# A quarter-row block of the query weights loaded onto 28 partitions by chosen DMA engines

## The chip, the cores and the metric

The kernel runs on one core of a Trainium2 chip. The time is device microseconds of one execution; three executions of the kernel before took 195.91, 196.07 and 196.13 us, median 196.07. A further execution was recorded by the hardware profiler; all times inside the kernel come from it, counted from its first instruction.

## The reference

One decode step of a gated mix of two blocks, for 4 batch rows with one token each, all in bf16:

```python
g = sigmoid((x * gate_w).sum(-1, keepdims=True))
q = (x @ wq)                     # 4 x 512 by 512 x 4096: 32 heads of 128
k, v = the last 4096 of 16384 cached rows, 8 heads, each for 4 query heads
o = softmax(q k^T * 128 ** -0.5) v
a = o @ wo                       # 4 x 4096 by 4096 x 512
b = (relu(x @ W_gate) * (x @ W_up)) @ W_down
return g * a + (1 - g) * b
```

Nearly all bytes are the caches: 32 pairs of batch row and cache head, each 4096 x 128 for K and again for V, 64 MiB in all. Weights add some 13 MiB. Each byte is read once and takes part in a few multiplications only.

## The kernel before

**Sets and slots.** The 32 pairs are done in eight sets of four heads of one batch row. A set's K and its V are one load of 4 MiB each, a partition holding 32 KB. Four slots of that size (`slots`, L109) are used in turn by every large load: query weights, K 0, K 1, V 0, K 2, V 1 and so on, then the gate and up weights together, V 7, the down weights and the output weights. `_dma_order` (L159) lists the loads and `_slots` (L166) gives each its slot and the event that frees it: the last transpose of a K, the last matmul of a V, the second half of the query matmuls for the query weights.

**Queues.** SyncE (SP) issues every load, in that order, on one queue (`sync`, L252); it waits where a slot is not free yet. A load of 128 partitions is spread over the core's sixteen DMA engines, eight partitions each, and every engine takes its part of the queue's loads one after the other. A load counts as landed when all its engines' parts have. The output weights come in five pieces (`WO_PIECES`, L28) that get smaller, so that the last matmuls can follow the last bytes closely. The fifth, 512 bytes a partition, is cut by `LOW3` (L29) into partitions 0 to 122, 123 to 125 and 126 to 127, which makes three transfers of it.

**The order of the work.** `_order` (L147) is one list that every compute engine follows, each through its own part. Ahead of the sets:

- GpSimd (POOL) builds identity matrices, masks and folding matrices, each step waiting for the one before (L287).
- VectorE (DVE) clears the block-diagonal query buffer `qblk` and the PSUM banks (`INIT`, L485).
- TensorE (PE) makes three constants from POOL's, then transposes x and the gate vector, five rows in all, in four pieces of 128 (`XT`, L333). Row 4p+t of the query weights sits on partition p as its t-th quarter, hence the step of four in the transposes.
- `Q` (L344): the query matmuls, two halves of 2048 columns. A half is four blocks of 512 columns times four t, accumulated over t into one PSUM bank, and the four blocks go to the rows from 0, 32, 64 and 96 of that bank.
- The queries are then copied, transposed and put into `qblk` (`EQ`, `QT`, `EQT`).

Within a set DVE transposes K in four fills (`EKT`, L489), PE multiplies them by the queries (`SC`), DVE adds the mask and keeps maxima, ScalarE (ACT) takes the exponential, DVE transposes it, and PE multiplies by V (`PV`). At the end come the second block (`GU`, `FFN`), the folding of the heads (`OQ`) and the output matmuls piece by piece (`WO`, L424): piece p is x from lo to hi, one matmul of 256 columns each. Two copies (`FIN` of ACT and of DVE) and one store end the kernel.

Of the kernel before, what the change touches and what calls it, by code (L numbers as in the profile page):

```python
# [24 lines left out]
OUTT = 2  # L25
OW = 512 // OUTT
OR = 128 // OUTT
WO_PIECES = ((0, 34), (34, 52), (52, 60), (60, 63), (63, 64))  # L28
LOW3 = (0, 123, 126, 128)  # L29

class _Plan:

# [70 lines left out]
def _alloc(nc, ctx):  # L103
    R = {}

    def sb(name, shape, dt):
        R[name] = ctx.enter_context(nc.sbuf_tensor(name, shape, dt))

    sb("slots", [128, NSLOT, 16384], BF16)  # L109
    sb("kt", [128, 4, 4096], BF16)  # L110
    sb("sc", [128, 2048], BF16)
    sb("pe", [128, 2048], BF16)
    sb("pT", [128, 2, 2048], BF16)
    sb("qblk", [128, NSET, 2, 144, 2], BF16)
    sb("xsb", [5, 512], BF16)
    sb("xT", [128, 20], BF16)
    sb("osb", [128, NSET, 512], BF16)
    sb("oq", [128, 32, 4], BF16)
    sb("identb", [128, 128], BF16)
    sb("identf", [128, 128], FP32)  # L120
    sb("ones", [128, 128], FP32)
    sb("ee", [16, 128], BF16)
    sb("e4", [16, 128], BF16)
    sb("rfold", [128, 128], FP32)
    sb("grpb", [128, 128], BF16)
    sb("own8", [128, 8], FP32)
    sb("scl", [128, 8], FP32)
    sb("maskl", [128, 128], BF16)
    sb("maskr", [128, 512], BF16)
    sb("maskf", [128, 512], BF16)  # L130
    sb("gwB", [128, 4, 128], BF16)
    sb("fold", [128, 4, 4, 64], BF16)
    sb("mx4", [128, 4], FP32)
    sb("rd32", [128, 8, 4], BF16)
    sb("negmax", [128, 2], FP32)
    sb("rowsum", [128, NSET], FP32)
    sb("recip", [128, 4, 4], FP32)
    sb("ge", [128, 2, 4], FP32)
    sb("gp", [128, 2, 4], FP32)
    sb("gg", [128, 2, 4], FP32)  # L140
    sb("hg", [128, 14, 4], BF16)
    sb("osum", [4, 512], BF16)
    R["psum"] = ctx.enter_context(nc.psum_tensor("bank", [128, 8, 512], FP32))
    return R
# [12 lines left out]


def _dma_order():  # L159
    o = [("wq",), ("x",), ("gw",), ("k", 0), ("k", 1), ("v", 0)]  # L160
    for s in range(2, NSET):
        o += [("k", s), ("v", s - 1)]
    return o + [("wg",), ("wu",), ("v", NSET - 1), ("wd",)] + [("wo", p) for p in range(len(WO_PIECES))]


def _slots():  # L166

    frees = [[] for _ in range(NSLOT)]
    at, wait = {}, {}
    turn = 0  # L170
    for it in _dma_order():
        k = it[0]
        if k in ("x", "gw") or (k == "wo" and it[1] > 0):
            continue
        if k == "wu":
            at[it] = at[("wg",)]
            wait[it] = wait[("wg",)]
            continue
        n = turn % NSLOT
        turn += 1  # L180
        at[it] = n
        wait[it] = list(frees[n])
        frees[n] = {"k": [("E", "KT", it[-1], 3)], "v": [("PV", it[-1])], "wq": [("Q", 1)], "wg": [("GU", 1)], "wd": [], "wo": []}[k]
    return at, wait


def _program(nc, plan, R, aps):
# [14 lines left out]
    def slot(*it):  # L202
        return slots[:, at[it], :]

    Wq = slot("wq").rearrange("p (t f) -> p t f", t=4)
    Wg, Wu = slot("wg")[:, 0:4 * FF], slot("wg")[:, 4 * FF:8 * FF]
    Wd = slot("wd")[:, 0:14 * 512]
    Wo = slot("wo", 0)
# [26 lines left out]
    def scb(key):  # L235
        return SCB[scf[key] % NSC]
# [2 lines left out]
        n = scf[key] - NSC  # L239
        return [("E",) + sck[n]] if n >= 0 else [("INIT",)]  # L240

    def wo_rows(p):

        return [slice(a, b) for a, b in zip(LOW3, LOW3[1:])] if p == len(WO_PIECES) - 1 else [slice(0, 128)]

    def set_of(s):
        return s % 4, s // 4
# [4 lines left out]
    def sync(e):  # L252
        E = _Eng(plan, e, "sp")

        def load(ev, ctr, dst, src, waits=()):
            E.op(lambda: e.dma_start(dst, src), ev=ev, waits=waits, ctr=ctr)  # L256

        for it in _dma_order():
            k = it[0]
            w = slot_wait.get(it, [])  # L260
            if k == "x":
                load(("X",), "d_x", xsb[0:4, :], A_x.rearrange("b o d -> (b o) d"))
            elif k == "gw":
                load(("GW",), "d_gw", xsb[4:5, :], gate_w.rearrange("(o p) -> o p", o=1))
            elif k == "wq":
                load(("WQ",), "d_wq", slot("wq"), A_wq.rearrange("(p t) f -> p (t f)", t=4), waits=w)
            elif k == "wg":
                load(("WG",), "d_wg", Wg, B_W_gate.rearrange("(p t) f -> p (t f)", t=4), waits=w)
            elif k == "wu":
                load(("WU",), "d_wu", Wu, B_W_up.rearrange("(p t) f -> p (t f)", t=4), waits=w)  # L270
            elif k == "wd":
                load(("WD",), "d_wd", Wd, B_W_down.rearrange("(p i) c -> p (i c)", i=14),
                     waits=w)
            elif k == "wo":
                lo, hi = WO_PIECES[it[1]]
                wo = A_wo.rearrange("(p i) c -> p (i c)", i=32)
                for n, r in enumerate(wo_rows(it[1])):
                    load(("WO", it[1], n), f"d_wo{it[1]}", Wo[r, OW * lo:OW * hi], wo[r, OW * lo:OW * hi], waits=w)
            else:
                b, qq = set_of(it[1])  # L280
                src = (A_k_cache if k == "k" else A_v_cache)[b, 4 * qq:4 * qq + 4, SK - WIN:SK, :]
                load((k.upper(), it[1]), f"d_{k}{it[1] % 3}", slot(*it), src.rearrange("h (r c) d -> r h (c d)", r=32),
                     waits=w)
        load(("OUT",), "d_out", out.rearrange("b o d -> (b o) d"), osum[:, :], waits=[("OSUM", 1), ("OSUM", 0)])
        E.wait([("OUT",)])

    def gpsimd(e):  # L287
# [7 lines left out]
        def aff(dst, src, pattern, base, cmp, fill, ev, mult=1):  # L295
            op(lambda: e.affine_select(dst, src, pattern, cmp, fill, base=base, channel_multiplier=mult), ev)  # L296
# [2 lines left out]
        op(lambda: e.memset(ones[:, :], 1.0), ("ONES",))  # L299
        aff(identf[:, :], ones[:, :], [[-1, 128]], 0, eq, 0.0, ("IDF",))  # L300
        aff(identb[:, :], ones[:, :], [[-1, 128]], 0, eq, 0.0, ("IDB",))
        aff(R["ee"][:, :], ones[0:16, :], [[0, 8], [-1, 16]], 0, eq, 0.0, ("EE",))
        aff(R["e4"][:, :], ones[0:16, :], [[0, 2], [-1, 16], [0, 4]], 0, eq, 0.0, ("E4",))
        op(lambda: e.memset(R["maskl"][:, :], -BIG), ("ML0",))
# [11 lines left out]
    def tensor(t):  # L316
# [16 lines left out]
        def XT():  # L333
            bk = bankb[tr(("XT",))]
            for q in range(4):
                tp(bk[:, 6 * q:6 * q + 5], xsb[0:5, q:q + 509:4], identb[0:5, 0:5], ev=("XT",) if q == 3 else None,
                   waits=tr_free(("XT",)) + [("X",), ("GW",), ("IDB",)])

        def Z():
            for q in range(4):  # L340
# [3 lines left out]
        def Q():  # L344
            for n in range(2):
                key = ("Q", n)
                for q in range(4):
                    for j in range(4):
                        c = (4 * n + j) * 512
                        mm(banks[scb(key)][32 * j:32 * j + 4, :], xT[:, 5 * q:5 * q + 4], Wq[:, q, c:c + 512],  # L350
                           q == 0, q == 3, ev=key if (q, j) == (3, 3) else None, pos=(0, 32 * j),
                           waits=sc_free(key) + [("WQ",), ("E", "XT"), ("INIT",)] if (q, j) == (0, 0) else ())

        def QT():
            for n in range(2):
# [67 lines left out]

        def WO(p):  # L424
            lo, hi = WO_PIECES[p]
            w = [("WO", p, n) for n in range(len(wo_rows(p)))] + [("E", "OQ")]
            for x in range(lo, hi):
                i, j = x // OUTT, x % OUTT
                mm(banks[ACC][OR * j:OR * j + 4, 0:OW], oq[:, i, :], Wo[:, OW * x:OW * x + OW], False, i == 31,
                   ev=("WOP", p) if x == hi - 1 else None, waits=w if x == lo else (), pos=(0, OR * j))  # L430

# [6 lines left out]
    for it in order:  # L438
# [3 lines left out]
        elif k == "CONST":  # L442
            act.append(("ECONST", it[1]))
        elif k == "XT":
            dve.append(("EXT",))
            act.append(("GWB",))
        elif k == "Z":
            act.append(("GE",))
# [33 lines left out]
    def vector(v):  # L482
        E = _Eng(plan, v, "dve")

        def INIT():  # L485
            E.op(lambda: v.memset(qblk[:, :, :, :, :].rearrange("p s h c e -> p (s h c e)"), 0.0), ev=("QZ",))  # L486
            E.op(lambda: v.memset(R["psum"][:, SCB[0]:ACC + 1, :].rearrange("p k c -> p (k c)"), 0.0), ev=("INIT",))

        def EKT(s, f):  # L489
            w = [("K", s)] + ([("SC", s - 1, f)] if s else [])  # L490
            E.op(lambda: v.transpose(kt[:, f, :].bitcast(FP32), slot("k", s)[:, 4096 * f:4096 * f + 4096].bitcast(FP32)),  # L491
                 ev=("E", "KT", s, f), waits=w)

        def EXT():
            E.op(lambda: v.tensor_copy(xT[:, :].rearrange("p (q c) -> p q c", q=4), bankb[tr(("XT",))][:, 0:24].rearrange("p (q c) -> p q c", q=4)[:, :, 0:5]), ev=("E", "XT"), waits=[("XT",)])  # L495

        def EQ(n):
            key = ("Q", n)
# [77 lines left out]
        def FIN():  # L576
            E.op(lambda: v.tensor_copy(osum[:, OW:2 * OW], banks[ACC][OR:OR + 4, 0:OW]), ev=("OSUM", 1),  # L577
                 waits=[("WOP", len(WO_PIECES) - 1)])

        fns = dict(INIT=INIT, EKT=EKT, EXT=EXT, EQ=EQ, G=G, EQT=EQT, ESC=ESC, MAX=MAX, ESW=ESW, EPT=EPT, ERS=ERS, EOQ=EOQ, H=H,  # L580
                   EHT=EHT, FIN=FIN)
        for it in dve:
            fns[it[0]](*it[1:])
# [75 lines left out]
```

## Time and profile before

| What | us |
|---|---|
| median of three executions | 196.07 |
| the profiled execution's own time | 196.06 |
| its span, first to last instruction | 194.8 |
| DVE busy | 124.1 |
| PE busy | 120.6 |
| ACT busy | 27.5 |
| POOL busy | 9.5 |

The span is what the profile covers; the remaining 1.26 us of the profiled execution lie around it. Busy times are sums over an engine's instructions. The page cuts the span into 40 slices of 4.87 us and gives each a digit for the busy share in tenths; the DMA row is the mean over the sixteen engines. Where a window is asked for, the same share is given as a fraction, so that one engine of sixteen counts 0.06. A line of the timeline has start, duration, engine, line, operation, what is written and read, and in brackets the idle time before and what ended it. A line of the waits has who waited, for whom, the time in total, how many times, and the longest.

### The profile page before, as it was taken

Reading aid. Unit: us, or ns where it says so; the run is one execution under the profiler, and the core shown is the slowest. Engines: PE = TensorE matmul, PEld = TensorE weight load, DVE = VectorE, ACT = ScalarE, POOL = GpSimd, SP = SyncE. Lnnn points to the kernel's source line nnn. Section 1 sums busy time; section 2 is a strip of 40 time slices with the busy share of each in tenths; the row PEclk is TensorE's granted clock in tenths of the full one; section 3 lists DMA queues with packets and bytes.
Section 4 is the critical chain, followed back from the end, with each engine's and each line's share of the span. In section 5 each row is a group of like instructions: output and inputs, shape, how many; then the busy total and the mean of one; then the engine's idle time right before and its main releaser. Section 6 shows DMA issues by size and latency. Waiting matters only on the chain.

```text
span 194.8 us, 1734 instructions
## 1 busy us (share of the span) xinstructions
PE 120.6 (62%) x723; PEld 50.6 (26%) x723; DVE 124.1 (64%) x153; ACT 27.5 (14%) x34; POOL 9.5 (5%) x25
## 2 busy tenths in 40 slices
PE   0209279474943894686468943894586466743974
PEld 0003123121411341242112411341142122311562
DVE  6103769999399809980998199819981998370010
ACT  2213000040130013001300130013001300420100
POOL 7830000000000000000000000000000000000000
PEclk9999958999999797899876999697999889997899
DMA  6999999999999999999999999999999999999992
GB/s 215 431 432 431 437 437 431 431 427 451 431 437 437 446 427 424 431 437 431 431 431 431 427 424 437 444 437 431 431 431 421 431 395 427 470 431 384 425 404 90
DMA packets 3616, 81.10 MB, mean 416 GB/s; under 512 B 401, under 2 KB 666, under 8 KB 794
## 3 DMA queue, kind: packets, MB, share of 16 engines
q1 hardware_dynamic: 3610, 81.01, 97.3%
q8 instruction: 5, 0.08, 0.2%
q14 instruction: 1, 0.01, 0.0%
HBM read 81.01 MB, written 0.00 MB: 416 GB/s over the span
## 4 chain that ended last, share of the span: by engine, by line
DMA 54%; DVE 31%; PE 9%; issue 4%; SPq 0%; ACT 0%
DMA slots<-in_A_k_cache_dram 38%; DVE kt L491 21%; DMA slots<-in_A_wo_dram 10%; PE bank L320 7%; DMA xsb<-in_A_x_dram 6%; DVE sc L527 5%; DVE qblk L517 1%; PE bank L324 1%; DVE pT L542 1%; DVE rd L531 1%; SPq L256 0%; DVE negmax L537 0%; ACT gwB L600 0%; DVE osum L577 0%; DVE mx L527 0%
## 5 line engine op out<-in xcount | busy, mean ns | idle before, releaser
L491 DVE STREAM_TRANSPOSE kt<-slots 128x2048 f32<-128x2048 f32 x32 | 73.7, 2305 | 28.1 <-DMA slots<-in_A_k_cache_dram 28.0
L320 PE MATMUL bank<-kt,qblk 128*128 128x512 bf16 x256 | 72.1, 434 | 27.9 <-DVE kt L491 27.9
L320 PEld LDWEIGHTS bank<-kt,qblk 128*128 128x128 bf16 x256 | 25.2, 107 | 69.7 <-DVE kt L491 36.0
L320 PE MATMUL bank<-slots,pT 128*64 128x512 bf16 x256 | 32.3, 410 | 5.7 <-DMA slots<-in_A_v_cache_dram 5.7
L619 ACT ACTIVATE pe<-sc,negmax 128x2048 bf16<-128x2048 bf16 x8 | 16.0, 2002 | 60.1 <-DVE negmax L537 60.1
L527 DVE CUSTOM_DVE_ANT_0 sc<-bank,maskf 128x512 bf16<-128x512 f32 x32 | 21.0, 658 | 3.8 <-PE bank L320 3.7
L320 PEld LDWEIGHTS bank<-slots,pT 128*64 128x64 bf16 x256 | 15.1, 118 | 23.2 <-issue 13.4
L542 DVE STREAM_TRANSPOSE pT<-pe 128x2048 bf16<-128x2048 bf16 x8 | 18.5, 2312 | 2.2 <-ACT pe L619 2.2
L604 ACT ACTIVATE osb<-bank 128x512 bf16<-128x512 f32 x8 | 4.8, 597 | 81.5 <-PE bank L320 81.5
L320 PE MATMUL bank<-rd,grpb 128*128 128x32 bf16 x8 | 1.6, 194 | 22.1 <-DVE rd L531 22.1
L555 DVE TENSOR_TENSOR oq<-bank,recip 64x128 bf16<-64x128 f32 x2 | 0.9, 434 | 12.3 <-PE bank L320 12.2
L320 PEld LDWEIGHTS bank<-rd,grpb 128*128 128x128 bf16 x8 | 0.8, 98 | 25.7 <-DVE rd L531 25.7
L495 DVE COPY xT<-bank 128x20 bf16<-128x20 bf16 x1 | 0.2, 171 | 8.0 <-PE bank L324 8.0
L320 PE MATMUL bank<-slots,oq 128*4 128x256 bf16 x64 | 4.0, 272 | 2.0 <-DMA slots<-in_A_wo_dram 2.0
L320 PE MATMUL bank<-slots,xT 128*4 128x512 bf16 (+1 forms) x64 | 5.0, 467 | 0.0
L320 PE MATMUL bank<-maskr,maskl 128*128 128x512 bf16 x1 | 0.6, 609 | 5.9 <-POOL maskr L296 5.9
L517 DVE TENSOR_SCALAR qblk<-bank 32x64 uint32<-32x64 uint32 x16 | 2.9, 215 | 2.1 <-PE bank L324 2.1
L324 PE MATMUL bank<-identb,xsb 5*128 5x5 bf16 x4 | 0.3, 168 | 5.7 <-DMA xsb<-in_A_x_dram 5.7
L577 DVE CAST osum<-bank 4x256 bf16<-4x256 f32 x1 | 0.4, 418 | 5.2 <-PE bank L320 5.2
L320 PEld LDWEIGHTS bank<-slots,oq 128*4 128x4 bf16 x64 | 2.5, 84 | 3.5 <-DMA slots<-in_A_wo_dram 2.9
L296 POOL TENSOR_SCALAR_AFFINE_SELECT fold<-fold 128x256 bf16<-128x256 bf16 x8 | 3.3, 417 | 1.1
L486 DVE MEMSET qblk<- 128x2304 uint32 x1 | 2.0, 1978 | 1.3 <-PEq L644 1.3
(59 smaller groups left out, 40.3 us busy)
## 6 DMA issues: line engine op xcount, KB each, us to landing
slots<-in_A_k_cache_dram SPq DMA_DIRECT2D x8, 4096.0 KB, 25.1
slots<-in_A_v_cache_dram SPq DMA_DIRECT2D x8, 4096.0 KB, 30.5
slots<-in_A_wq_dram SPq DMA_DIRECT2D x1, 4096.0 KB, 12.4
slots<-in_A_wo_dram SPq DMA_DIRECT2D x1, 2176.0 KB, 17.1
slots<-in_B_W_gate_dram SPq DMA_DIRECT2D x1, 1792.0 KB, 19.7
slots<-in_B_W_up_dram SPq DMA_DIRECT2D x1, 1792.0 KB, 23.6
slots<-in_B_W_down_dram SPq DMA_DIRECT2D x1, 1792.0 KB, 18.5
slots<-in_A_wo_dram SPq DMA_DIRECT2D x1, 1152.0 KB, 19.5
```

The costliest lines, as they stand in the source:

```text
L296: op(lambda: e.affine_select(dst, src, pattern, cmp, fill, base=base, channel_multiplier=mult), ev)
L320: E.op(lambda: t.matmul(out_, lhsT, rhs, start=start, stop=stop, tile_position=pos, skip_group_check=True), ev=ev, waits=waits)
L324: E.op(lambda: t.transpose(out_, in_, idn), ev=ev, waits=waits)
L486: E.op(lambda: v.memset(qblk[:, :, :, :, :].rearrange("p s h c e -> p (s h c e)"), 0.0), ev=("QZ",))
L491: E.op(lambda: v.transpose(kt[:, f, :].bitcast(FP32), slot("k", s)[:, 4096 * f:4096 * f + 4096].bitcast(FP32)), ev=("E", "KT", s, f), waits=w)
L517: E.op(lambda dst=dst, r=r, g=g: v.tensor_scalar(dst, src[r, g, 0:B, :, :], 0, None, op0=ALU.bitwise_or), ev=("E",) + keys[1] if (q, g) == ...
L527: E.op(lambda: v.tensor_tensor_reduce(sc[:, 512 * f:512 * f + 512], banks[scb(key)], R["maskf"][:, :], 1.0, -3.0e38, ALU.add, ALU.max, mx4 ...
L531: E.op(lambda: v.tensor_tensor(rd32[:, :, :], bc(R["own8"][:, :].unsqueeze(2), 2, 4), bc(mx4[:, :].unsqueeze(1), 1, 8), ALU.mult), ev=("MA ...
L542: E.op(lambda: v.transpose(pT[:, s % 2, :], pe[:, :]), ev=("E", "PT", s), waits=[("EXP", s)] + ([("PV", s - 2)] if s >= 2 else []))
L555: E.op(lambda g=g, r=r: v.tensor_tensor(oq[r, :, :].rearrange("p i b -> p b i"), banks[tr(key)][0:64, 128 * g:128 * g + 128].rearrange("p ...
L604: E.op(lambda: a.activation(osb[:, s, :], ob(s), ACTF.Copy), ev=("NORM", s), waits=[("PV", s)])
L619: E.op(lambda: a.activation(pe[:, :], sc[:, :], ACTF.Exp, bias=negmax[:, s % 2:s % 2 + 1], scale=SCALE, accum_out=rowsum[:, s:s + 1]), ev= ...
```

## The change

The query weights' quarter t=3 (row 4p+3 on partition p) no longer brings its columns 3072 to 4095 with the large load, which now moves 15360 of 16384 elements a partition. These 128 rows of 1024 columns come in three loads of their own into the slot of V 0, which is free then: 48 rows onto partitions 32 to 43 (four on each), 40 onto partitions 60 to 67 and 40 onto 112 to 119 (five on each). SP issues the first; GpSimd issues the other two, each behind a small load into scratch (`TURN`, on 28 and on 12 partitions, 128 bytes each) that is not used by any computation. The part of the slot that the matmuls read is cleared by DVE first, and all three loads wait for that.

Rows now lie on other partitions than in the large load, so x has to be laid out to match: three DVE copies (`XG`) put the elements of x into `xg`, and five more transposes bring them into 25 further columns of `xT`. In the second half of `Q` the two blocks of columns from 3072 on leave out t=3 and add five matmuls each over the rows laid out anew. V 0's load waits for the second half of `Q` and for the `TURN` loads, since it overwrites what they use. The fifth output piece is no longer cut in three: it is one load over all partitions.

```diff
--- before.py
+++ after.py
+SIDE_F = 3072
+SIDE = ((0, 3, 4, 0, 32), (1, 2, 5, 48, 60), (2, 2, 5, 88, 112))
 WO_PIECES = ((0, 34), (34, 52), (52, 60), (60, 63), (63, 64))
-LOW3 = (0, 123, 126, 128)
...
-    sb("xT", [128, 20], BF16)
+    sb("xT", [128, 45], BF16)
+    sb("xg", [5, 5, 128], BF16)
...
-    o = [("wq",), ("x",), ("gw",), ("k", 0), ("k", 1), ("v", 0)]
+    o = [("wq",), ("x",), ("gw",), ("side",), ("k", 0), ("k", 1), ("v", 0)]
...
+    wait[("v", 0)] = wait[("v", 0)] + [("Q", 1), ("TURN", 1)]
...
+    side = slot("v", 0)[:, 0:5 * 1024].rearrange("p (j f) -> p j f", j=5)
+    scratch = slot("v", 0)[:, 6 * 1024:6 * 1024 + 128]
...
-    def wo_rows(p):
-
-        return [slice(a, b) for a, b in zip(LOW3, LOW3[1:])] if p == len(WO_PIECES) - 1 else [slice(0, 128)]
+    def side_of(n):
+
+
+        _, e, j, p, q = SIDE[n]
+        src = A_wq.rearrange("(p t) f -> p (t f)", t=4)[p:p + 4 * e * j, 3 * 4096 + SIDE_F:4 * 4096]
+        return side[q:q + 4 * e, 0:j, :], src.rearrange("(r e) f -> e r f", e=e)
+
+    def side_x(n):
+
+        _, e, j, p, q = SIDE[n]
+        src = xsb[0:5, 4 * p:4 * p + 16 * e * j].rearrange("p (r j e t) -> p j e r t", r=4, j=j, e=e, t=4)[:, :, :, :, 3]
+        return R["xg"][0:5, 0:j, q:q + 4 * e].rearrange("p j (e r) -> p j e r", e=e), src
...
-                load(("WQ",), "d_wq", slot("wq"), A_wq.rearrange("(p t) f -> p (t f)", t=4), waits=w)
+                load(("WQ",), "d_wq", slot("wq")[:, 0:3 * 4096 + SIDE_F],
+                     A_wq.rearrange("(p t) f -> p (t f)", t=4)[:, 0:3 * 4096 + SIDE_F], waits=w)
+            elif k == "side":
+                load(("SIDE", 0), "d_side0", *side_of(0), waits=[("SZ",)])
...
-                for n, r in enumerate(wo_rows(it[1])):
-                    load(("WO", it[1], n), f"d_wo{it[1]}", Wo[r, OW * lo:OW * hi], wo[r, OW * lo:OW * hi], waits=w)
+                load(("WO", it[1]), f"d_wo{it[1]}", Wo[:, OW * lo:OW * hi], wo[:, OW * lo:OW * hi], waits=w)
...
         aff(identb[:, :], ones[:, :], [[-1, 128]], 0, eq, 0.0, ("IDB",))
+        rows = A_wo.rearrange("(p i) c -> p (i c)", i=4)
+        for n, k in ((1, 7), (2, 3)):
+            src = rows[0:4 * k, 0:64].rearrange("(r e) c -> e r c", e=k)
+            E.op(lambda n=n, k=k, src=src: e.dma_start(scratch[0:4 * k, 64 * n - 64:64 * n], src), ev=("TURN", n - 1), ctr="d_turn")
+            E.op(lambda n=n: e.dma_start(*side_of(n)), ev=("SIDE", n), waits=[("SZ",)], ctr=f"d_side{n}")
...
-                tp(bk[:, 6 * q:6 * q + 5], xsb[0:5, q:q + 509:4], identb[0:5, 0:5], ev=("XT",) if q == 3 else None,
+                tp(bk[:, 6 * q:6 * q + 5], xsb[0:5, q:q + 509:4], identb[0:5, 0:5], 
                    waits=tr_free(("XT",)) + [("X",), ("GW",), ("IDB",)])
+            for j in range(5):
+                tp(bk[:, 6 * (4 + j):6 * (4 + j) + 5], R["xg"][0:5, j, :], identb[0:5, 0:5], ev=("XT",) if j == 4 else None,
+                   waits=[("XG",)])
...
-                for q in range(4):
-                    for j in range(4):
...
+                steps = [(q, j) for q in range(4) for j in range(4) if (4 * n + j) * 512 < SIDE_F or q < 3]
+                sides = [(q, j) for q in range(5) for j in range(4) if (4 * n + j) * 512 >= SIDE_F]
...
+                for q, j in sides:
+                    c = (4 * n + j) * 512 - SIDE_F
+                    mm(banks[scb(key)][32 * j:32 * j + 4, :], xT[:, 20 + 5 * q:24 + 5 * q], side[:, q, c:c + 512],
+                       False, q == 4, ev=key if (q, j) == sides[-1] else None, pos=(0, 32 * j),
+                       waits=[("SIDE", g) for g in range(3)] if (q, j) == sides[0] else ())
...
-            w = [("WO", p, n) for n in range(len(wo_rows(p)))] + [("E", "OQ")]
+            w = [("WO", p), ("E", "OQ")]
...
         def INIT():
+            E.op(lambda: v.memset(side, 0.0), ev=("SZ",))
+            E.op(lambda: v.memset(R["xg"][:, :, :], 0.0), ev=("XGZ",))
...
+        def XG():
+            for n in range(3):
+                E.op(lambda n=n: v.tensor_copy(*side_x(n)), ev=("XG",) if n == 2 else None, waits=[("X",), ("GW",), ("XGZ",)])
```

More of the change, by code (lines that the diff above doesn't have):

```diff
@@ L172, in _slots @@
         k = it[0]
-        if k in ("x", "gw") or (k == "wo" and it[1] > 0):
+        if k in ("x", "gw", "side") or (k == "wo" and it[1] > 0):
             continue
@@ L346, in Q @@
                 key = ("Q", n)
-                for q in range(4):
-                    for j in range(4):
[L349 to L352, printed above, removed]
+                steps = [(q, j) for q in range(4) for j in range(4) if (4 * n + j) * 512 < SIDE_F or q < 3]
+                sides = [(q, j) for q in range(5) for j in range(4) if (4 * n + j) * 512 >= SIDE_F]
+                for q, j in steps:
+                    c = (4 * n + j) * 512
+                    mm(banks[scb(key)][32 * j:32 * j + 4, :], xT[:, 5 * q:5 * q + 4], Wq[:, q, c:c + 512],
+                       q == 0, q == 3, ev=key if (q, j) == steps[-1] and not sides else None, pos=(0, 32 * j),
+                       waits=sc_free(key) + [("WQ",), ("E", "XT"), ("INIT",)] if (q, j) == (0, 0) else ())
+                for q, j in sides:
[3 more added lines that the diff above has]
+                       waits=[("SIDE", g) for g in range(3)] if (q, j) == sides[0] else ())
         def QT():
@@ L444, in _program @@
         elif k == "XT":
-            dve.append(("EXT",))
+            dve += [("XG",), ("EXT",)]
             act.append(("GWB",))
@@ L492, in EKT @@
                  ev=("E", "KT", s, f), waits=w)
+        def XG():
+            for n in range(3):
+                E.op(lambda n=n: v.tensor_copy(*side_x(n)), ev=("XG",) if n == 2 else None, waits=[("X",), ("GW",), ("XGZ",)])
         def EXT():
-            E.op(lambda: v.tensor_copy(xT[:, :].rearrange("p (q c) -> p q c", q=4), bankb[tr(("XT",))][:, 0:24].rearrange("p (q c) -> p q c", q=4)[:, :, 0:5]), ev=("E", "XT"), waits=[("XT",)])
+            E.op(lambda: v.tensor_copy(xT[:, :].rearrange("p (q c) -> p q c", q=9), bankb[tr(("XT",))][:, 0:54].rearrange("p (q c) -> p q c", q=9)[:, :, 0:5]), ev=("E", "XT"), waits=[("XT",)])
         def EQ(n):
@@ L578, in FIN @@
                  waits=[("WOP", len(WO_PIECES) - 1)])
-        fns = dict(INIT=INIT, EKT=EKT, EXT=EXT, EQ=EQ, G=G, EQT=EQT, ESC=ESC, MAX=MAX, ESW=ESW, EPT=EPT, ERS=ERS, EOQ=EOQ, H=H,
+        fns = dict(INIT=INIT, XG=XG, EKT=EKT, EXT=EXT, EQ=EQ, G=G, EQT=EQT, ESC=ESC, MAX=MAX, ESW=ESW, EPT=EPT, ERS=ERS, EOQ=EOQ, H=H,
                    EHT=EHT, FIN=FIN)
```

## The prediction

> **What bounds the kernel now.** I began with the page: the DMA engines' busy share by slices of the span, and the queues.
>
> ```profile
> DMA  6999999999999999999999999999999999999992
> q1 hardware_dynamic: 3610, 81.01, 97.3%
> q8 instruction: 5, 0.08, 0.2%
> q14 instruction: 1, 0.01, 0.0%
> HBM read 81.01 MB, written 0.00 MB: 416 GB/s over the span
> ```
>
> The sixteen engines are full from first slice to last; 81.01 MB are 5.06 MB an engine, and the trace's steady packets of 32 KB take 1213 ns, so 187.5 us of the 194.8 are transfer. Compute matters only where it starves the queue or stands behind the last byte. SP's own waits say the first does not happen:
>
> ```profile
> SPq L256 <- DVE kt L491: 120.5, 8, 16.4
> SPq L256 <- PE bank L320: 38.5, 8, 14.1
> ```
>
> SP stands long before a free slot, yet a K load lands 25.1 us and a V load 30.5 us after its issue (medians on the page), where 4 MB take 9.7: some 15 us of older loads are always queued. So the end decides. The table of windows there (PE, its loads, DVE, ACT, POOL; then TensorE's clock, DMA share, GB/s):
>
> ```profile
> 190.40:190.60 0.20, 0.00 (x0) 0.00 (x0) 0.00 (x0) 0.00 (x0) 0.00 (x0) 1.00 0.68 254
> 191.60:191.80 0.20, 0.20 (x8) 0.08 (x2) 0.00 (x0) 0.00 (x0) 0.00 (x0) 1.00 0.37 138
> 191.80:192.00 0.20, 0.17 (x4) 0.00 (x0) 0.00 (x0) 0.00 (x0) 0.00 (x0) 1.00 0.13 46
> ```
>
> A share of 0.37 is six engines of sixteen: ten are done and six still work. The trace's landing records agree. Each load lands in sixteen parts; of the third output piece (`WO_PIECES[2]`) ten land from 190.20 to 190.71 us, six from 191.45 to 192.16; of the fourth, ten from 190.70 to 191.23, six from 191.88 to 192.60. The fifth lies on three engines (rows cut by `LOW3`) and lands at 192.39. The timeline of the end shows what follows:
>
> ```profile
> 192.20 0.82 PE L320 MATMUL bank<-slots,oq 128*4 128x256 bf16 x12 [0.23 <-DMA slots<-in_A_wo_dram]
> 193.06 0.37 ACT L623 ACTIVATE osum<-bank 4x256 bf16<-4x256 f32 x1 [8.90 <-PE bank L320]
> 193.09 0.42 DVE L577 CAST osum<-bank 4x256 bf16<-4x256 f32 x1 [5.16 <-PE bank L320]
> 193.54 0.27 SPq L256 DMA_DIRECT2D out_dram<-osum  x1
> ```
>
> Eight matmuls on piece three start when it lands; the ninth starts at 192.64, just after piece four (192.60); the last at 192.75, then the copy and the store, 2.06 us to the end at 194.81.
>
> Why six are late: the DMA view of a stretch around an instruction packet (queue 8, 16 KB).
>
> ```profile
> q1 hardware_dynamic: 16, 0.49, 106.2%
> q8 instruction: 1, 0.02, 6.0%
> ```
>
> 6.0% of sixteen engines is one engine for the whole 1.1 us. The packet records show the load queue of one engine silent for 1.03 us there, and its next packet 1694 ns instead of 1213: 1.5 us lost where 16 KB should cost 0.61. There are five such packets (40.2, 73.0, 111.7, 148.2, 182.1 us), each on another engine, and an 8 KB packet on queue 14 at 63.3 us that costs 0.97. That makes the six.
>
> [...]
>
> **The change, part by part.** Columns 3072 to 4095 of row set t=3 (256 KB) leave the query load: each engine has 8 partitions x 2 KB = 16 KB less, 1213/16 x 8 = 0.61 us. They come back as 128 rows of 2 KB: 48 by SP on three engines[...], 16 each; 40 by GpSimd on two engines, 20 each, and again 40 on two. [...]the small `TURN` loads (7 engines, 3 engines) place these on engines 7, 8 and 12, 13.
>
> A 2 KB packet is not in the trace. Neighbours: 1536 bytes step by 61 ns, 4096 by 159; on the line between, 2 KB is 81 ns[...]. So +1.30 us on the three engines, +1.62 on the four.
>
> The fifth output piece goes from three lanes of 41 packets (about 1 us) to 8 packets of 23 to 27 ns on each engine: +0.21 us everywhere.
>
> Sums, at the landing of the last piece (fourth now, fifth then):
> - Nine engines without a share: -0.61 + 0.21 = -0.40. If the six late ones are among them, 192.60 becomes 192.20.
> - Three low engines: 190.70 to 191.23 - 0.61 + 1.30 + 0.21, 191.6 to 192.13.
> - Four engines, if early ones: + 1.22, 191.9 to 192.45.
>
> After the fifth piece only one matmul is left, started 0.04 us later. Now it starts at 192.75; then at 192.24 to 192.49. Gain 0.26 to 0.51 us; I take 0.42.
>
> The unknown is the cost of GpSimd's queue cutting into the load queue.[...] Lower bound zero[...]; upper, per turn, the fetch's excess: 1.5 - 0.61 = 0.9, or 0.97 - 0.30 = 0.67 for the 8 KB one; a line through both leaves 0.4 for a turn alone. I take near 0[...], and keep 0.9 once or per packet for the range. A gain from it is excluded: it adds bytes.
>
> The rest, against the start of the timeline:
>
> ```profile
> 0.80 0.40 SPq L256 DMA_DIRECT2D slots<-in_A_wq_dram  x1
> 1.35 1.98 DVE L486 MEMSET qblk<- 128x2304 uint32 x1 [1.35 <-PEq L644]
> 4.30 1.57 POOL L296 TENSOR_SCALAR_AFFINE_SELECT maskr<-maskr 128x512 bf16<-128x512 bf16 x1
> 13.23 0.27 PE L324 MATMUL bank<-identb,xsb 5*128 5x5 bf16 x4 [5.72 <-DMA xsb<-in_A_x_dram]
> 18.00 0.54 SPq L256 DMA_DIRECT2D slots<-in_A_k_cache_dram  x1
> ```
>
> - Zeroing `side`: 2560 words at 1978/2304 ns are 2.2 us, `xg` 0.3. SP waits for it until 3.6 us; behind that wait stand SIDE 0, K0, K1. The query load runs until 11 us, so it is covered; without cover it would be 2.5. DVE's bank clear ends near 8.1 instead of 5.5, still before x lands.
> - POOL: two `TURN`s and two shares, a wait for the zeros ahead of each share.[...] Queued behind: the mask matmul, ACT's copies, then XT. x lands near 12.6, so little or nothing[...].
> - XG: three small DVE copies, 0.4 us; five transposes, 0.3; eight query matmuls more at 0.107, 0.86. Q ends near 19.5, not 18.0.
> - V0, issued at 3.2 us before, now waits for Q and `TURN`; K2 stands behind it on SP and waited for Q already (18.00). The queue holds query, K0 and K1 until 31.6 us, so about 11 us are free. DVE's first set starts 1.5 us later, against 15 us of queued loads. All nothing.
> - Two output issues fewer on SP: nothing, they wait for the queue.
>
> The profiled execution took 196.06 us, span 194.8 and 1.26 around it, the median 196.07; so 196.07 - 0.42 = 195.65.
>
> **The rivals.**
> 1. *The forecast*, 195.5 to 195.9. For it: six late engines that set the end, ten with 1.4 us to spare. Against: nothing in the profile names the late engines by number.
> 2. *One turn costs what a fetch costs beyond its bytes*, 0.4 to 0.9, on late engines too through `TURN`: 192.20 to 192.45 become 192.6 to 193.35, the last matmul moves by -0.1 to +0.65: 196.0 to 196.7.
> 3. *The shares fall on late engines*, slower: [...]the fetches lie on 7, 8, 12 or 13. Then 192.60 + 1.22 = 193.82, last matmul +1.1, with a turn +1.9: 197.2 to 198. It decides as soon as one of the four is late; the overload breaks even at 0.1 us beyond 192.60.
> 4. *A turn per packet*: at two rows a packet ten turns of 0.4 to 0.9, 4 to 9 us on four engines: 199.5 to 205. If turns come per row, a share needs 20 x 1.2 us beside query and K0 packets, lands near 30, Q is late and V0 too: the queue runs dry at 31.6.
> 5. *It does not do what it says*: GpSimd spreads its rows over all sixteen, 10 KB each: -0.61 + 0.40 + 0.21 = 0 on the late engines: 196.0.
>
> **How the numbers follow.** Chances 0.40, 0.22, 0.14, 0.18, 0.06. About 0.2% (0.39 us) is what a measurement of this kernel can tell. Faster: 0.27 of case 1. Same: 0.13 of case 1, 0.13 of case 2, case 5: 0.32. Slower: 0.09 of case 2, cases 3 and 4: 0.41. The range 195.5 to 197.6 leaves out case 4 and the top of 3; case 1's own is 195.5 to 195.9. As gain and loss share the chances, the likeliest case's time is the forecast.
>
> **What would show it.** The late six should land the last piece near 192.2, four others at 191.9 to 192.45, and the DMA share should fall in one step, not in two. A GpSimd queue of 80 rows of 2 KB should appear, with 40 small packets for `TURN`. 32 KB packets much over 1213 ns before 25 us mean cases 2 or 4; a last landing past 193.5 with the early engines unmoved means 3; K2 or V0 issued after 25 us means late shares. I am wrong if the instruction packets change in number or engine, or if the end is set by anything but the last landing.

## The result and the profile after

The changed kernel takes 205.69 us (median of six executions, 205.05 to 207.02); the kernel before, 196.11 (195.91 to 196.40). The ratio is 1.0497, with a 95% interval from 1.0461 to 1.0532: some 9.6 us slower. The profiled execution took 205.47 us, its span is 204.2, so 1.3 us lie around it as before.

The page of the kernel after, its row of DMA shares and its queues:

```profile
DMA  7999991699999699999999999999999999998992
q1 hardware_dynamic: 3669, 80.85, 93.2%
q0 software_dynamic: 416, 0.17, 0.3%
q8 instruction: 6, 0.10, 0.2%
q14 instruction: 1, 0.01, 0.0%
```

The row of before was full from the second slice to the last but one. Here slice 7 has a 1 and slices 8 and 14 a 6: twice the sixteen engines have nothing to do, near 33 and near 68 us. The load queue q1 falls from 97.3 to 93.2% of the engines' span. The new queue q0 is GpSimd's.

The table of windows around both gaps, in columns as in the prediction (PE, its loads, DVE, ACT, POOL; then TensorE's clock, DMA share, GB/s):

```profile
31.00:32.00 1.00, 0.00 (x0) 0.00 (x0) 0.00 (x0) 0.00 (x0) 0.00 (x0) 1.00 0.50 205
32.00:34.00 2.00, 0.01 (x2) 0.04 (x2) 0.00 (x0) 0.00 (x0) 0.00 (x0) 1.00 0.06 25
34.00:36.00 2.00, 2.00 (x10) 0.48 (x10) 0.00 (x0) 0.00 (x0) 0.00 (x0) 1.00 0.00 0
37.00:38.00 1.00, 0.91 (x6) 0.68 (x4) 0.05 (x1) 1.00 (x1) 0.00 (x0) 1.00 0.70 197
67.00:68.00 1.00, 1.00 (x4) 0.32 (x3) 0.95 (x1) 0.00 (x0) 0.00 (x0) 0.50 0.16 66
68.00:69.00 1.00, 1.00 (x8) 0.29 (x8) 0.39 (x1) 0.00 (x0) 0.00 (x0) 0.90 0.00 0
```

From 32 to 37 us the DMA engines move next to nothing; PE works only from 34. A share is, here and below, one of the loads of the moved rows. The timeline says what PE waited for and what waited for PE:

```profile
33.99 2.30 PE L341 MATMUL bank<-slots,xT 128*4 128x512 bf16 x10 [15.66 <-DMA slots<-in_A_wq_dram]
36.32 0.53 SPq L270 DMA_DIRECT2D slots<-in_A_v_cache_dram  x1
36.90 0.60 SPq L270 DMA_DIRECT2D slots<-in_A_k_cache_dram  x1
42.10 4.50 DVE L523 STREAM_TRANSPOSE kt<-slots 128x2048 f32<-128x2048 f32 x2
67.98 0.54 SPq L270 DMA_DIRECT2D slots<-in_A_k_cache_dram  x1
```

Before, V 0's issue and the first transpose stood here:

```profile
3.22 0.62 SPq L256 DMA_DIRECT2D slots<-in_A_v_cache_dram  x1
23.23 2.31 DVE L491 STREAM_TRANSPOSE kt<-slots 128x2048 f32<-128x2048 f32 x1
```

The ten query matmuls over the shares start at 33.99, after PE has stood still for 15.66 us. V 0 and K 2 are issued when they are done, at 36.3 and 36.9 us; before, V 0 went out at 3.2 and K 2 at 18.0. The queue held query weights, K 0 and K 1, and these have landed by 33.7. K 3 at 67.98 waits for the first sets' transposes, which now start at 42.1 instead of 23.2; V 1 lands at 67.71 to 69.28, so most engines are idle again.

The landing records give the sum of it. By the mean over its sixteen parts, K 1 lands 0.46 us later than before, V 0 6.36, V 1 6.55, K 3 8.86, the fourth output piece 9.19; the last landing of all moves from 192.60 to 202.12, by 9.5. So 5.9 us are lost in the first gap, 2.3 in the second and under half a microsecond ahead of both; 0.3 more is added between K 3 and the fourth output piece.

Why the shares are late is in the packet records. These name no engine; which packets belong to one engine is read from their steps and counts. GpSimd's rows come as packets of 4 KB, two rows each, that take 159 ns. In the first share two series of ten stand 0.25 us apart, one for each of its two engines. One of them starts at 8.42, 9.71, 11.00, 12.29, 12.45, 13.82, 15.18, 16.55, 17.91 and 19.27 us. Between two of these there is room for one packet of 30 or 32 KB of the load queue (1138 or 1213 ns) and no more; only the fifth follows the fourth at once, where the query weights end. The same queue shows 280 packets of 8 bytes, in step with them. By their number that is one on each of the fourteen other engines at each of the ten steps of either share (14 x 20). The second share's first packet starts at 21.89, when the first share is through, although it lies on other engines, and its last at 33.28. The semaphore records say the same: the first share lands at 21.37, the second at 33.86.

### The profile page after: what moved, and what is told of

Read it like the earlier page. It is cut to its first block, busy times and chain, and to the rows that moved or that the text cites. A ratio compares the mean times of both kernels' runs of the same rounds, so it can differ in the third digit from the quotient of the medians.

```text
span 204.2 us, 1771 instructions
## 1 busy us (share of the span) xinstructions
PE 126.0 (62%) x736; PEld 52.0 (25%) x736; DVE 127.8 (63%) x158; ACT 27.5 (13%) x34; POOL 12.2 (6%) x29
## 3 DMA queue, kind: packets, MB, share of 16 engines
q1 hardware_dynamic: 3669, 80.85, 93.2%
## 4 chain that ended last, share of the span: by engine, by line
PE 37%; DVE 31%; DMA 22%; issue 8%; POOL 1%; SPq 0%
PE bank L341 36%; DVE kt L523 19%; DMA slots<-in_A_wq_dram 14%; DMA slots<-in_A_wo_dram 8%; DVE sc L563 6%; DVE qblk L553 1%; PE bank L345 1%; DVE pT L578 1%; DVE slots L516 1%; DVE rd L567 1%; DVE negmax L573 1%; POOL slots L322 0%; POOL slots L321 0%; SPq L270 0%; DVE osum L613 0%
## 5 line engine op out<-in xcount | busy, mean ns | idle before, releaser
L341 PE MATMUL bank<-slots,pT 128*64 128x512 bf16 x256 | 33.5, 421 | 2.2 <-DMA slots<-in_A_v_cache_dram 2.2
L341 PE MATMUL bank<-slots,xT 128*4 128x512 bf16 (+1 forms) x72 | 7.6, 504 | 15.7 <-DMA slots<-in_A_wq_dram 15.7
L341 PEld LDWEIGHTS bank<-slots,xT 128*4 128x4 bf16 x72 | 2.1, 101 | 19.8 <-issue 19.2
L626 ACT ACTIVATE sc<-bank 128x2048 bf16<-128x2048 f32 x1 | 1.9, 1877 | 21.2 <-PE bank L341 21.2
L528 DVE COPY xg<-xsb 5x40 bf16<-5x40 bf16 (+1 forms) x3 | 0.5, 199 | 4.2 <-DMA xsb<-in_A_x_dram 4.2
```

The source lines that it names most:

```text
L341: E.op(lambda: t.matmul(out_, lhsT, rhs, start=start, stop=stop, tile_position=pos, skip_group_check=True), ev=ev, waits=waits)
```

## Experiments

Theory A: each 4 KB packet of a share waits for one whole load packet, the two shares stand one behind the other, so the last lands at 33.9 us; the query matmuls are late, V 0 and K 2 too, and the queue runs dry. Theory B: the turns (an engine's change to the other queue for one packet, and back) slow the engines themselves, whatever the length of the packets.

**Smaller load packets, everything else as changed.** The query load and K 0 are cut along the row, in halves in the first kernel and in quarters in the second. The edit of the query load in halves; K 0 is cut the same way:

```diff
-                load(("WQ",), "d_wq", slot("wq")[:, 0:3 * 4096 + SIDE_F],
-                     A_wq.rearrange("(p t) f -> p (t f)", t=4)[:, 0:3 * 4096 + SIDE_F], waits=w)
+                for a in range(0, 4 * 4096, 16384 // 2):
+                    z = min(a + 16384 // 2, 3 * 4096 + SIDE_F)
+                    load(("WQ",) if z == 3 * 4096 + SIDE_F else ("WQ", a), "d_wq", slot("wq")[:, a:z],
+                         A_wq.rearrange("(p t) f -> p (t f)", t=4)[:, a:z], waits=w)
```

> The changed kernel, with the query load and K 0 each cut into two loads of half a row, so that the load queue's packets are 16 and 14 KB instead of 30 and 32 until about 21 us. Theory A (each 4 KB packet of GpSimd's shares waits for one whole load packet, the two shares stand one behind the other, so the third share lands at 33.9 us, the query matmuls are late and the load queue runs dry): the 22 or so turns take 0.6 to 0.75 us each instead of 1.2 to 1.3, the last share lands at 22 to 25 us, the queue never runs dry, and the time falls from 205.7 to 195.5 to 196.3 us. Theory B (the second queue's turns themselves slow the engines, whatever the packet size): the time stays at 203 us or more.

> As the half-row kernel, but in quarters (8 and 6 KB packets until about 21 us). Theory A: 22 turns of about 0.4 us, the last share lands at 16 to 19 us, no dry queue; the smaller packets themselves cost up to 0.5 us (4 KB packets step by 159 ns in the trace of before, 4.8% over the 32 KB rate; a quarter row should lose about half of that over 20 us), so 195.8 to 196.6 us. Theory B: 203 us or more, or worse than the half-row kernel, since there are more changes between the queues.

Halves: 197.34 us (196.58 to 197.89), ratio 1.0058 (1.0037 to 1.0080). Quarters: 197.67 us, ratio 1.0080 (1.0065 to 1.0096). The last share lands at 23.47 and 17.11 us, inside both expectations. The row of DMA shares on the half-row kernel's page:

```profile
DMA  6999999999999999999999999999999999999991
```

And its timeline:

```profile
23.61 1.44 PE L346 MATMUL bank<-slots,xT 128*4 128x512 bf16 x6 [4.75 <-DMA slots<-in_A_wq_dram]
25.94 0.53 SPq L270 DMA_DIRECT2D slots<-in_A_v_cache_dram  x1
```

No gap is left, V 0 goes out at 25.94, and 8.3 of 9.6 us are back, with the same bytes, the same 40 and 280 packets of GpSimd's queue and the same added copies and matmuls. As the cause of the loss theory B is out. The time itself missed theory A's range, by 1.0 us for both; what remains follows below.

**Lateness alone, without any share.** On the kernel before, the query matmuls wait for K 1 and V 0 for the query matmuls:

```diff
+    wait[("v", 0)] = wait[("v", 0)] + [("Q", 1)]
...
-                           waits=sc_free(key) + [("WQ",), ("E", "XT"), ("INIT",)] if (q, j) == (0, 0) else ())
+                           waits=sc_free(key) + [("WQ",), ("E", "XT"), ("INIT",), ("K", 1)] if (q, j) == (0, 0) else ())
```

> The kernel before, with no share and no GpSimd load: only the query matmuls wait for K 1 to land (about 32 us) and V 0's load waits for the second half of the query matmuls. Theory A: this lateness alone makes the loss; V 0 is issued near 35.7 us instead of 3.2, the queue is dry from about 32 to 37 us and again near 67 us, and the time is 203.5 to 206 us. Theory B: the loss is in the queues' turns, so lateness alone costs less than 3 us: 196 to 199 us.

205.62 us, ratio 1.0492 (1.0458 to 1.0527): the loss of the change, without any of its loads. Windows of this kernel, columns as above:

```profile
32.00:34.00 2.00, 1.28 (x16) 0.46 (x20) 0.00 (x0) 0.00 (x0) 0.00 (x0) 1.00 0.00 0
34.00:36.00 2.00, 2.00 (x24) 0.52 (x16) 1.32 (x3) 0.00 (x0) 0.00 (x0) 1.00 0.00 0
68.00:69.00 1.00, 1.00 (x10) 0.48 (x10) 0.72 (x3) 0.00 (x0) 0.00 (x0) 1.00 0.08 33
```

And SP in its timeline:

```profile
36.35 0.54 SPq L257 DMA_DIRECT2D slots<-in_A_v_cache_dram  x1
67.70 0.54 SPq L257 DMA_DIRECT2D slots<-in_A_k_cache_dram  x1
```

V 0 and K 3 leave at 36.35 and 67.70, within 0.3 us of the changed kernel, and the same two gaps follow.

**The added wait of V 0 alone.** Only the first of the two lines above:

> The kernel before, with V 0's load waiting for the second half of the query matmuls as in the change, and nothing else changed: V 0 issued near 18 us. Theory A: no effect, since query weights, K 0 and K 1 fill the queue to 31.6 us: 195.9 to 196.3 us. Rival (the added wait alone makes the gap): 200 us or more.

196.20 us, ratio 1.0004 (0.9995 to 1.0012), V 0 issued at 18.29. The wait cost nothing here, with the query matmuls on time. Late query matmuls without this wait were not tried, so how much of the loss needs both is open.

**Half the share.** The changed kernel with load packets uncut and shares of 512 columns (`SIDE_F` 3584, the width of `side` 512):

> The changed kernel with shares of 512 columns instead of 1024 (rows of 1 KB), load packets uncut. Theory A (the delay is the number of 4 KB packets that each wait for a load packet): 5 turns a share instead of 10, the last share lands at 21 to 25 us instead of 33.9, the queue never runs dry, and without the cut packets' cost the time is 195.9 to 196.6 us: late engines lose 0.30 us and get 0.21 for the fifth piece and some 0.15 for the second queue, loaded ones stand about 1 us behind the others instead of 2. Theory A with a fixed delay instead of one by packets: last share still near 30 us and 203 us or more.

197.53 us (197.10 to 198.16), ratio 1.0073 (1.0056 to 1.0091). The last share lands at 24.82 us instead of 33.86, inside the expectation. There are half as many 4 KB packets, in the second share still 1.40 us apart on each engine (1.38 in the changed kernel). The two shares themselves take 11.8 us instead of 22.5; the pause between them, 2.9 us here and 2.4 there, does not shrink. So the delay goes with the number of packets (this run halves their bytes with it). The time missed, by some 0.9 us. V 0 is out at 27.28, but K 3 only at 59.32, and K 3's first part lands 0.80 us later than before where that of V 1 was 0.12 later: a short second gap is still there (from 60 to 61 us the DMA share is 0.69). A further 0.62 us had been lost by K 1.

**What the moved bytes should have brought.** With the delay gone, the half-row kernel is still 0.58% slower. Two parts of it alone, on the kernel before: the fifth piece whole (`LOW3 = (0, 128)`), and the query load and K 0 in halves without any share.

> The kernel before with the fifth output piece as one load over all partitions, as in the change, and nothing else. By the prediction's term the late engines' last landing moves from 192.60 to 192.81, three matmuls of 0.055 us earlier in the chain are gained: +0.05 to +0.3 us, so 196.1 to 196.4. If the piece was no help on the low engines: 195.9 to 196.1.

> The kernel before with the query load and K 0 cut into halves of a row, no shares. 512 packets of 617 ns instead of 256 of 1213: 5 us over sixteen engines, +0.3 us: 196.3 to 196.6. If cut packets cost nothing, 196.1, and the whole 1.25 us of the half-row kernel is the shares'; if they cost 1 us or more, 197.1, the shares' balance was hidden by them.

196.04 us, ratio 0.9996 (0.9987 to 1.0005), and 196.11 us, 0.9998 (0.9990 to 1.0006). Neither costs anything that can be measured; both lie under the first ranges expected of them (196.1 to 196.4 and 196.3 to 196.6). The whole fifth piece lands 0.19 us after the fourth, close to the 0.21 of the prediction, and one matmul instead of three or four is left then. Cut packets leave K 1's mean landing at 32.26 (32.25 before), so the 0.3 us that I had given them was wrong.

So the half-row kernel's rest comes with the shares and their queue. Its landings of K 1, in order, a bar between nine and seven:

```
31.92 32.05 32.07 32.07 32.10 32.11 32.14 32.20 32.40 | 33.32 33.44 33.67 33.77 34.04 34.26 34.42
```

Nine engines stand at 32.12 in the mean, seven at 33.85. Against 32.25 before, the unloaded nine gained 0.13 us where the prediction took 0.61, and the loaded seven lost 1.60 where it had 0.69 (three) and 1.01 (four). The mean over all is 0.63 later, and still 0.62 at the fourth piece. There the last part is 1.30 later (193.89 against 192.60), the first 0.04 earlier.

**Which engines.** Two series of fifteen tiny loads on 1, 2, ... 15 partitions number the engines: the one that joins in the load of k partitions is called engine k - 1. They go behind K 1 and behind the first output piece, on the kernel before and, twice, on the half-row kernel.

> The kernel before, with two series of fifteen tiny loads of their own ([...]each with a packet size that nothing else has), one behind K 1 and one behind the first output piece. They number the engines: the engine that shows up in the load of k partitions but not in that of k - 1 is engine k - 1. In the first series all sixteen should stand within 0.6 us. In the second some five or six should be about 1.5 us behind (0.97 for the one of the 8 KB packet). Theory C (rival 3 of the prediction): among these are engines 7, 8, 12 or 13. Theory D (the shares lie on engines that no instruction packet delays): none of 0, 1, 2, 7, 8, 12, 13 is. The time itself rises by the markers, 1 to 3 us, and says nothing.

> The half-row kernel with the same two series. First series: engines 0, 1, 2, 7, 8, 12, 13 behind the others by 1.3 to 1.6 us[...]. Second series: theory C says that at least one engine has both delays and stands 2.7 to 3.2 us behind; theory D says that none is more than 2.0 us behind and that the loss comes from somewhere else.

> The same kernel as the half-row one with markers, a second execution, to see whether the numbers hold.[...] If the instruction packets keep to their engines, 3, 5, 6, 9, 10, 11 have the delay as in the first execution; if they move, one of the loaded engines may stand 3 us behind.

The times (199.51, 200.39 and 200.01 us) hold the markers' own cost. First series of the half-row kernel, against its median: engines 0, 1, 2, 7, 8, 12, 13 are 1.6 to 2.2 us behind, all others within 0.3; the second execution gives the same seven, 1.3 to 2.3. The expectation had 1.3 to 1.6. Four of the seven are those that the prediction names for GpSimd's shares, and three are the lowest, in both executions; in the trace of the changed kernel SP's share lands in three parts (13.91 to 14.11 us) and the `TURN` loads have seven and three packets of 512 bytes. That these two loads are what brings the shares to 7, 8, 12 and 13 was the author's assumption: the numbers fit it, and no run leaves the loads out. From first to second series (us beyond the least delayed; the markers cost low numbers up to 2 us, so neighbours are compared; engine 15 has no marker):

```
engine             3    4    5    6    7    8    9    10   11   12   13   14
before            2.42 1.32 2.85 2.58 0.94 0.38 1.82 1.61 0.09 0.09 0.00 1.52
half row          2.52 1.42 2.94 2.69 1.01 0.47 2.46 1.70 1.85 0.00 0.01 0.28
half row, again   2.61 1.48 2.62 2.70 0.97 0.32 1.91 1.62 1.61 0.00 0.01 0.02
```

Five engines stand 1.1 to 2.0 us beyond the nearest one without such a delay, which fits a 16 KB instruction packet on each: 5, 6, 9, 10 and, before, 14; in the half-row kernel 11 takes the place of 14. Engine 3 has a smaller delay, 1.1 us beyond engine 4, which fits the 8 KB packet. The four that GpSimd loads are on time in all three, so theory D holds there. It does not hold in every execution: in the profile of the half-row kernel without markers the parts of K 5 stand at most 2.39 us behind the first, those of V 4 at 3.29. The value 1.74, one of the seven loaded engines', is gone from the list and 3.29 is new: the instruction packet at 117 us fell on a loaded engine. This may explain the wide span of that kernel's times, 196.58 to 197.89; which of the other executions had it is not known.

**The second queue alone.** The kernel before, with GpSimd's four loads in size and order of the change into spare memory:

```diff
+        for n, k in ((1, 7), (2, 3)):
+            src = rows[0:4 * k, 0:64].rearrange("(r e) c -> e r c", e=k)
+            share = rows[40 * n:40 * n + 40, 0:1024].rearrange("(r e) c -> e r c", e=2)
+            E.op(lambda n=n, k=k, src=src: e.dma_start(R["turn"][0:4 * k, 64 * n - 64:64 * n], src), ev=("TURN", n - 1), ctr="d_turn")
+            E.op(lambda n=n, s=share: e.dma_start(R["spare"][:, n - 1, :], s), ev=("SPARE", n), ctr=f"d_spare{n}")
```

> The kernel before, with GpSimd's four loads of the change in the same sizes and order (28, 40, 12 and 40 rows), into spare memory that nothing reads; nobody waits for them but the end. It adds 160 KB of loads that the change only moves, and takes nothing from the query load. Question: what does a second queue cost the engines that carry none of its data? The half-row kernel's K 1 landings suggest 0.36 to 0.45 us on each of the twelve: then their K 1 landing is at 32.4 to 32.7 us instead of 32.25, and the four loaded ones stand 1.5 to 2.2 us behind those. With the query matmuls at their old place the queue does not run dry: the loaded engines land the fourth piece at 192.5 to 193.3 and the time is 196.3 to 197.2 us. If the second queue is free for the others, they land K 1 at 32.2 to 32.3.

198.94 us (198.26 to 199.70), ratio 1.0154 (1.0115 to 1.0193), above the expectation. Here the second queue is not free for engines without data: twelve land K 1 at 33.6 to 34.7 us, 1.4 to 2.4 later than 32.25, not 0.2 to 0.45. The 32 KB packets between two turns take 1284 to 1306 ns (medians of 4 us stretches from 10 to 34) where they take 1213 in the kernel before. In the changed kernel the same stretches show 1213 to 1231. So a turn cost up to some 20 ns there and 70 to 95 here, on top of the 9 ns of an 8-byte packet. These shares go to 40 partitions of 2 KB instead of eight of 10 and wait for no zeros, the query load is whole, and V 0 stands in the queue already; which of these makes the difference was not tried.

## Why the prediction was wrong

**The bound and the cause of the six late engines** held. The loss in the transfers shows in the time one to one (the fourth piece's mean landing 9.2 us later, 8.2 of it in the gaps before V 0 and K 3; the time 9.6), and the markers find five engines with the delay of an instruction packet and one with the smaller delay.

**The step that failed** is the end of the query matmuls in "The rest": its third item has "Q ends near 19.5, not 18.0", from added compute alone, and its fourth builds on it: "The queue holds query, K0 and K1 until 31.6 us, so about 11 us are free ... All nothing." The 31.6 was nearly right (K 1 lands at 31.86 to 33.71). The 19.5 was not: the matmuls ended at 36.3. The forecast priced the shares as engine time, 20 x 81 ns, and that was right (ten packets of 159 ns); it gave them no time of arrival. The packets that a share's packets wait for were in the trace of before: 32 KB, 1213 ns each. Twenty data packets, one load packet ahead of each, and the second share behind the first give 20 x 1.25 = 25 us from 8.4, that is 33.4; the last landed at 33.9. This sum, made afterwards, comes so close by some luck: most steps were 1.29 to 1.38 us, a few packets followed another at once, and 2.4 us lay between the shares. The half-row and quarter-row kernels remove the loss of the gaps, and late query matmuls alone, with V 0 behind them, reproduce it.

**Rival 4** named the place, and its upper end of 205 us lies near the measured 205.7 by luck, since it comes from another sum. Its 4 to 9 us were turns that cost the four engines 0.4 to 0.9 each; in the changed kernel a turn costs at most some 20 ns, and 9 ns more for a packet of 8 bytes. The dry queue was its last sentence, for turns per row only. With packets of two rows I took ten turns and did not see that the second share runs behind the first, which makes ten into twenty. The price of an instruction packet beyond its bytes (0.9 us), my upper bound for a turn, does not carry over.

**The other rivals.** Rival 2's 0.4 to 0.9 us for a turn is not found in the two kernels where the turns were timed (0.1 us at most), and against rival 5 the markers find the rows on the engines named. Rival 3 does not show in the marked executions; the profiled execution of the half-row kernel has it once, and its 197.42 us lie in the 197.2 to 198 of that rival, though share and queue cost more there than the rival had.

**The turn near zero** in the forecast was close for one turn and wrong in sum: over some 24 turns the nine unloaded engines of the half-row kernel kept only 0.13 of 0.61 us.

**The balance** (-0.40 on late engines, 192.20) is not seen in the changed kernel at all. At the first gap all engines wait for V 0 together: K 1's parts lie 1.84 us apart, V 0's 0.33, so the head start of the unloaded engines is gone before the end comes. Four engines are then late by instruction packets, 201.58 to 202.12 against 200.40 to 200.72. Where the gap is absent, in the half-row kernel, the loaded engines are the late ones: 1.7 us behind the others, more than the 1.4 us that the early engines had to spare. The terms for share and queue were both too small. Of the share's, one part is measured: in the changed kernel SP's 2 KB packets took 84 to 107 ns, where the prediction had 81.

**Right:** clearing `side` and `xg` took 2.19 and 0.33 us (2.2 and 0.3), SP went on at 3.63, `maskr` was ready at 10.0 behind GpSimd's four issues of 0.58 to 0.73 us each, ahead of x, which landed at 12.72 and whose transposes began at 12.81, the fifth piece's landing came 0.19 us after the fourth's, the shares lay on the engines named in both marked executions of the half-row kernel, and in the marked executions the four engines that GpSimd loads were among the early ones.

**The signs named** did their work: V 0 issued after 25 us was listed as the mark of late shares. Another came true without making the loss: the instruction packets changed in number (six on queue 8 instead of five) and, in the half-row kernel, in one engine. GpSimd's queue appeared with 40 packets of two rows, and ten of 512 bytes for `TURN`, where 80 and 40 were forecast.

## What to carry to other kernels

In these runs a small transfer on a second queue was served one packet for one packet against what the first queue had in flight: most packets of 4 KB, 159 ns each, came 1.29 to 1.38 us apart beside load packets of 1138 and 1213 ns, and the last share landed at 33.86 us beside whole load packets, at 23.47 beside halves and at 17.11 beside quarters. Its time of arrival came near the number of its packets times the length of the other queue's packets, with all that stood ahead of it on its own queue (33.4 us by the sum above), and not to its bytes over the bandwidth. Count both before something waits for it, and cut the long packets where it has to come through. In a kernel bound by transfers, ask of every new wait how many bytes are still queued behind it when it ends: V 0's wait for the query matmuls was free when these ended at 18 us, and together with their late end at 36 it cost 9.5.

## What was not expected of the hardware

- By their number, each of the two shares of GpSimd put 8-byte packets on the fourteen engines that carried none of it, one for each 4 KB packet of a loaded engine (280 = 14 x 20). The two shares, on different engines, ran one behind the other (8.4 to 19.5 and 21.9 to 33.4 us). That the 8-byte packets hold the second one back fits this and is not shown.
- Halving the load packets from 32 to 16 KB over 8 MB changed nothing that can be measured (K 1's mean landing 32.26 against 32.25 us, ratio 0.9998).
- An instruction packet of 16 KB cost the load queue of its engine about 1.5 us, and the engine that got it was not always the same: 14 in the kernel before with markers, 11 in the half-row kernel with markers, and without them once a loaded one.
- Still open: why the load queue's packets between two turns took 1213 to 1231 ns in one kernel and 1284 to 1306 in another.
